# Grouped-query attention with a KV cache: a reordered head, an earlier last K load, and a rearranged tail

## Chip, cores and metric

One core of one Trainium2 chip runs the whole program. The metric is the device time of one execution in microseconds (us). Of the 16 executions of before, 15 lie within 0.3% of their median and all within 0.53% of one another, so differences below one microsecond are read from five rounds. The before median was 391.56 us over 5 runs.

## The reference

```python
# x (32,4,1024); k_cache, v_cache (32,4,2048,128); wq (1024,4096); wo (4096,1024); all bf16
q = (x @ wq).reshape(B, Sq, 32, 128).transpose(0, 2, 1, 3)
k = jnp.repeat(k_cache, 8, axis=1)
v = jnp.repeat(v_cache, 8, axis=1)
p = softmax(einsum("bhqd,bhkd->bhqk", q, k) * 128 ** -0.5)
o = einsum("bhqk,bhkd->bhqd", p, v)
out = o.transpose(0, 2, 1, 3).reshape(B, Sq, 4096) @ wo
```

The caches are 134 MB of the 151 MB that must be read. The kernel works in 32 "quads": quad q is one KV head (q // 8) and four batch entries, with one K tile and one V tile of 2 MB each.

## The kernel before

SyncE issues all loads in one queue. The order of the issues, and what each issue waits for, decide when data arrives (with K31 sent ahead of V29 and nothing else changed, its transpose started at 358.15 us instead of 361.65):

```python
for g in range(Hkv): sp_wq(g)
sp_K(0)
for q in range(NQ):                 # NQ = 32
    if q + 1 < NQ: sp_K(q + 1)      # two raw K buffers: K(q) waits for transpose kx(q-2)
    sp_V(q)                         # four V buffers: V(q) waits for PV of quad q-4
    if q in wo_at: sp_Wo(wo_at[q])
sp_Wo(Hkv - 1)
```

VectorE transposes K (`kx`) and takes the row maximum (`mx`). In its program the transpose for the next quad stands ahead of the maximum of this one, and the trace shows them run in that order (the transpose of K31 from 361.65 us, the maximum of quad 30 from 366.02):

```python
dve_trK(0)
for g in range(1, Hkv): qsb{g}      # scales half of Q projection g out of PSUM
for k in range(NQ + 1):
    if k + 1 < NQ: dve_trK(k + 1)   # kx1 also waits for "qp3", the fourth projection
    if k < NQ:     dve_max(k); dve_negm(k)
    if k >= 1:     dve_lred(k - 1); dve_recip(k - 1)
    ...
```

TensorE runs, per step k: scores S(k), transposes of the probabilities PT(k-1), the product PV(k-1), and the transpose OT(k-2). In the tail there are "fillers", matmuls whose results nobody reads:

```python
pe_qproj(0)
for me in range(4): pe_qt_round(0, me)
for g in range(1, Hkv): pe_qproj(g)       # each needs the PSUM banks of the one before
TF = 12,5,1,1,1,1
for k in range(NQ + 2):
    if k == NQ - 1: pe_fill(TF[0])        # twelve fillers before S(31)
    pe_S(k); ...
    if k == NQ: pe_fill(TF[1])
    pe_PT(k-1, 0); pe_PT(k-1, 1); ...; pe_PV(k-1, 0); ...; pe_PV(k-1, 1); ...; pe_OT(k-2)
pe_proj(Hkv - 1, 0); pe_proj(Hkv - 1, 1)  # last Wo; VectorE then adds acc and writes out
```

(`...` and the shortened loops are cuts.)

Of the kernel before, what the change touches and what calls it, by code (L numbers as in the profile page):

```python
# [5 lines left out]
F32 = mybir.dt.float32  # L6
U32 = mybir.dt.uint32
ACTF = mybir.ActivationFunctionType
ALU = mybir.AluOpType
# [51 lines left out]
def bass_standalone__gqa_block_cached__sampling_kernel(  # L61
# [9 lines left out]
    _, Hkv, Sk, Dh = k_cache.shape  # L71
    HD = wq.shape[1]
    Hq = HD // Dh
    REP = Hq // Hkv
# [5 lines left out]
    NQP = B // 4  # L80
# [13 lines left out]
    def sbt(name, shape, dt):  # L94
        t = nc.sbuf_tensor(name, shape, dt)
        sb.append(t)
        return t.__enter__()

    ident = sbt("ident", [128, 128], BF)
    xT = sbt("xT", [128, NDT, 128], BF)  # L100
    Qsb = sbt("Qsb", [128, HD], BF)
    Qrep = sbt("Qrep", [128, 4, REP, 128], BF)
# [55 lines left out]
    PJ_ps = PS[:, 7168:8192].bitcast(F32)  # L158
    PJ6_ps = PS[:, 6144:7168].bitcast(F32)
    FILL_ps = PS[:, 6144:7168].bitcast(F32)  # L160

    sems = []

# [60 lines left out]
    def sp_K(q):  # L224
        slot = q % 2
        k_uses[slot] += 1
        b0, g = quad_b0(q), quad_g(q)

        def aps():
            src = k_cache[b0:b0 + 4, g, :, :].rearrange("j (p n) d -> p j (n d)", p=128)  # L230
            dst = Kraw[:, slot, :].rearrange("p (j x) -> p j x", j=4)
            return dst, src
        waits = []
        if q >= 2:
            waits.append(f"kx{q - 2}")
        sp_dma(aps, s_K[slot], f"K{q}", 16 * k_uses[slot], waits)

    def sp_V(q):
        slot = q % NV
        v_uses[slot] += 1  # L240
        b0, g = quad_b0(q), quad_g(q)

        def aps():
            src = v_cache[b0:b0 + 4, g, :, :].rearrange("j (p n) d -> p j (n d)", p=128)
            dst = Vs[slot].rearrange("p (j x) -> p j x", j=4)
            return dst, src
        waits = []
        if q >= NV:
            waits.append(f"o{q - NV}")
        if slot >= 2 and v_uses[slot] == 1:  # L250
            waits.append("qp3")
        sp_dma(aps, s_V[slot], f"V{q}", 16 * v_uses[slot], waits, engname=v_eng, qidx=q)

    def sp_Wo(g):
        semh = s_w[0]
        w_uses[0] += 1

        def aps():
            src = wo[REP * Dh * g:REP * Dh * (g + 1), :].rearrange("(h d) n -> d h n", d=Dh)
            dst = Wo  # L260
            return dst, src
        waits = ["qp3"]
        if g >= 1:
            waits.append(f"proj{g - 1}_1")
        sp_dma(aps, semh, f"wo{g}", 16 * w_uses[0], waits)

    wo_at = {4: 0, 13: 1, 21: 2}
    for g in range(Hkv):
        sp_wq(g)
    sp_K(0)  # L270
    for q in range(NQ):
        if q + 1 < NQ:
            sp_K(q + 1)
        sp_V(q)
        if q in wo_at:
            sp_Wo(wo_at[q])
    sp_Wo(Hkv - 1)

    def sp_final(eng):
# [27 lines left out]

    qrep_events = {g: [] for g in range(Hkv)}
    qrep_items = {"dve": [], "act": [], "pool": []}
    g0_assign = ["dve", "act", "pool", "pool"] * 4  # L310
    idx = 0
    for me in range(4):
        for c in range(4):
# [20 lines left out]
                                 fill=1.0, base=0, pattern=[[-1, 128]], channel_multiplier=1)  # L334
    S.add("pool", "ident0", pool_memset)
    S.add("pool", "ident", pool_ident)
    if V_ON_POOL:
        later = {1: [], 2: [], 3: []}
        for item in qrep_items_pool_later:
            later[int(item[0][4])].append(item)  # L340
        v_after = {1: qrep_items["pool"] + later[1], 9: later[2], 17: later[3]}
        for q in range(NQ):
            S.add("pool", *pool_v_items[q])
            for item in v_after.get(q, []):
                S.add("pool", *item)
    else:
        for item in qrep_items["pool"] + qrep_items_pool_later:
            S.add("pool", *item)
# [27 lines left out]
    def pe_qproj(g):  # L376
        prev = (bank_free_ev[0] or ()) + (bank_free_ev[1] or ())
        bank_free_ev[0] = bank_free_ev[1] = (f"qsb{g}_dve", f"qsb{g}_act")

        def f(eng):  # L380
            waits = ["xT_ev", f"wq{g}"] + list(prev)
            S.wait(eng, "pe", *waits)
            ins = None
            for dt in range(NDT):
                for n2 in range(2):
                    ins = eng.matmul(QP_ps[:, 512 * n2:512 * (n2 + 1)], xT[:, dt, :],  # L386
                                     wq_v[:, g, dt, 512 * n2:512 * (n2 + 1)],
                                     start=(dt == 0), stop=(dt == NDT - 1))
            return ins
        S.add("pe", f"qp{g}", f)  # L390
# [112 lines left out]

    fill_rhs = QT4[:, 0, 0, 0:512]

    def pe_fill(n):
        def f(eng):
            ins = None
            for i in range(n):
                ins = eng.matmul(FILL_ps, ident[:, :], fill_rhs, start=True, stop=True)  # L510
            return ins
        if n > 0:
            S.add("pe", None, f)

    pe_qproj(0)
    for me in range(4):
        pe_qt_round(0, me)
    for g in range(1, Hkv):
        pe_qproj(g)
    proj_at = {}  # L520
    for gg in range(1, Hkv):
        proj_at[NQP * gg + 2] = (gg - 1, 0)
        proj_at[NQP * gg + 3] = (gg - 1, 1)
    TF = [int(v) for v in _os.environ.get("GQA_TAILFILL", "12,5,1,1,1,1").split(",")]
    TF += [0] * (6 - len(TF))
    for k in range(NQ + 2):
        if k < NQ:
            if k == NQ - 1:
                pe_fill(TF[0])
            pe_S(k)  # L530
            if k in qt_round_after_S:
                gq, me = qt_round_after_S[k]
                pe_qt_round(gq, me)
        if 1 <= k <= NQ:
            if k == NQ:
                pe_fill(TF[1])
            pe_PT(k - 1, 0)
            pe_PT(k - 1, 1)
            if k == NQ:
                pe_fill(TF[2])  # L540
            pe_PV(k - 1, 0)
            if k == NQ:
                pe_fill(TF[3])
            pe_PV(k - 1, 1)
        if 2 <= k <= NQ + 1:
            if k == NQ + 1:
                pe_fill(TF[4])
            pe_OT(k - 2)
        if k in proj_at:
            pe_proj(*proj_at[k])  # L550
    pe_fill(TF[5])
    pe_proj(Hkv - 1, 0)
    pe_proj(Hkv - 1, 1)

    def dve_xT_ev(eng):
        S.wait(eng, "dve", "xT_tr")
# [15 lines left out]
    S.add("dve", "qsb0_dve", dve_qsb(0))  # L572
    for item in qrep_items["dve"]:
        S.add("dve", *item)
    S.add("act", "qsb0_act", act_qsb(0))
    for item in qrep_items["act"]:
        S.add("act", *item)
# [56 lines left out]
    def dve_acc(g, n2):  # L634
        def f(eng):
            waits = [f"proj{g}_{n2}"]
            if (g, n2) != (0, 0) and not (g == Hkv - 1 and n2 == 1):
                pg, pn = (g, 0) if n2 == 1 else (g - 1, 1)
                waits.append(f"acc{pg}_{pn}" if not (pg == Hkv - 1) else "fin0")
            if g == Hkv - 1 and n2 == 1:  # L640
                waits.append("fin0")
            S.wait(eng, "dve", *waits)
            a = acc[:, 512 * n2:512 * (n2 + 1)]
            src = PJ_ps if proj_bank(g, n2) == 7 else PJ6_ps
            if g == 0:
                return eng.tensor_copy(a, src)
            if g < Hkv - 1:
                return eng.tensor_tensor(a, a, src, ALU.add)
            return eng.tensor_tensor(out_sb[:, 512 * n2:512 * (n2 + 1)], a, src, ALU.add)
        if g == Hkv - 1:  # L650
            name = f"fin{n2}"
        else:
            name = f"acc{g}_{n2}"
        S.add("dve", name, f)

    dve_trK(0)
    for g in range(1, Hkv):
        S.add("dve", f"qsb{g}_dve", dve_qsb(g))
    acc_at = {}
    for gg in range(1, Hkv):  # L660
        acc_at[NQP * gg + 2] = (gg - 1, 0)
# [1 line left out]
    for k in range(NQ + 1):  # L663
# [7 lines left out]
            dve_recip(k - 1)  # L671
        if k in acc_at:
            dve_acc(*acc_at[k])
    dve_acc(Hkv - 1, 0)
    dve_acc(Hkv - 1, 1)

    def act_qtev(gq, me):
        slot = gq % 2
# [20 lines left out]
            return eng.activation(Osb[:, :], O_ps, ACTF.Copy, scale=st_rl(slot))  # L699
        S.add("act", f"on{q}", f)  # L700

    def act_evac(q, half):
        def f(eng):
            waits = [f"pt{'AB'[half]}{q}"]
            if q >= 1:
                waits.append(f"o{q - 1}")
            S.wait(eng, "act", *waits)
            src = B4v if half == 0 else B5v
            return eng.activation(PTsb[:, 8 * half:8 * half + 8, :], src, ACTF.Copy)  # L709
        S.add("act", f"pte{'AB'[half]}{q}", f)  # L710

    def act_exp(q, c):
        slot = q % 2
# [12 lines left out]
    def act_otev(q):  # L726
# [10 lines left out]
            return eng.activation(dst, src, ACTF.Copy)  # L737
        S.add("act", f"ote{q}", f)

    for me in range(4):  # L740
        act_qtev(0, me)
    for g in range(1, Hkv):
        S.add("act", f"qsb{g}_act", act_qsb(g))
    for k in range(NQ + 2):
        if 2 <= k <= NQ + 1:
            act_norm(k - 2)
        if 1 <= k <= NQ:
            act_evac(k - 1, 0)
            act_evac(k - 1, 1)
        if k < NQ:  # L750
            for c in range(4):
                act_exp(k, c)
            if k in qt_round_after_S:
                gq, me = qt_round_after_S[k]
                act_qtev(gq, me)
        if 2 <= k <= NQ + 1:
            act_otev(k - 2)

    S.plan()
    with nc.Block() as block:  # L760
# [53 lines left out]
```

## Time and profile before

| what | before |
|---|---|
| median time | 391.56 us |
| span of the profiled run | 389.7 us |
| moved by DMA | 152.21 MB, mean 391 GB/s |
| where DMA falls short | first 3.5 us; 49 to 51.5 us; from about 368 us |
| K30 transpose starts / K31 transpose starts | 351.38 / 361.65 us |
| last projection starts | 382.99 us |

First the page of the profile. The strips have 40 slices of the span each: the TensorE clock that was granted in tenths (9 means full, 5 means half) and the rate of the DMA. The last line is the head of the chain of waits.

```profile
span 389.7 us, 10775 instructions
...
PEclk9985955896555556965556668996656557955699
...
GB/s 304 410 418 410 410 320 414 418 407 415 416 416 413 409 413 417 416 408 408 417 422 415 408 415 418 415 408 410 419 422 412 408 414 420 416 409 413 385 111 29
...
DMA 65%; DVE 21%; PE 7%; SPq 2%; ACT 2%; issue 0%
```

The rate is near 410 in nearly every slice. The sixth slice (about 49 to 58 us) has 320, and the last two have 111 and 29. The chain says that 65% of the span is spent waiting for K loads. No slice moves more than 422. With the same bytes to move at that rate, this kernel can gain only by closing holes in the DMA and by shortening what follows the last loads.

The hole in detail. This is the table of busy times by stretches of one microsecond; the last two columns are the DMA's share and its GB/s.

```profile
core 0: us, PE busy (x) PEld busy (x) DVE busy (x) ACT busy (x) POOL busy (x), PEclk, DMA share, GB/s
...
48.00:49.00 1.00, 0.00 (x0) 0.00 (x0) 1.00 (x1) 0.00 (x0) 0.00 (x0) 1.00 1.04 414
49.00:50.00 1.00, 0.00 (x0) 0.00 (x0) 1.00 (x2) 0.00 (x0) 0.00 (x0) 0.83 0.09 25
50.00:51.00 1.00, 0.00 (x0) 0.00 (x0) 1.00 (x1) 0.00 (x0) 0.00 (x0) 0.50 0.00 0
51.00:52.00 1.00, 0.00 (x0) 0.00 (x0) 1.00 (x1) 0.00 (x0) 0.00 (x0) 0.50 0.79 270
...
```

What led to it is in the timeline (start, duration, engine, line, operation, then the idle time before it and who ended it). L587 is the K transpose, L386 a Q projection, L202 a load's issue.

```profile
29.26 4.45 DVE L587 STREAM_TRANSPOSE KX<-Kraw 128x4096 uint32<-128x4096 uint32 x1 [12.93 <-DMA Kraw<-in_k_cache_dram]
...
34.39 6.09 PE L386 MATMUL PS<-arena,xT 128*128 128x512 bf16 x16 [12.22 <-DVE Qsb L563]
...
41.30 3.61 PE L386 MATMUL PS<-arena,xT 128*128 128x512 bf16 x16 [0.83 <-DVE Qsb L563]
...
45.56 4.43 DVE L587 STREAM_TRANSPOSE arena<-Kraw 128x4096 uint32<-128x4096 uint32 x1
...
50.02 0.37 SPq L202 DMA_DIRECT2D Kraw<-in_k_cache_dram  x1
```

The second K transpose, at 45.56, was not late for want of data: K1 had landed at 34.4 us, as the landing records in the trace show (a load is split over 16 DMA engines, each with a record of its own; "landed" means that the last part is there). It waited for the fourth projection (41.30 to 44.9), which waited for the third, which waited for VectorE, which was transposing K0. K3 needed the buffer that the second transpose frees, and was issued at 50.02, when the queue had run dry.

The tail, again from the timeline. L598 is the maximum, L510 the fillers, L428 the scores, L498 the last projection.

```profile
351.38 4.45 DVE L587 STREAM_TRANSPOSE KX<-Kraw 128x4096 uint32<-128x4096 uint32 x1 [4.16 <-DMA Kraw<-in_k_cache_dram]
...
361.65 4.45 DVE L587 STREAM_TRANSPOSE arena<-Kraw 128x4096 uint32<-128x4096 uint32 x1 [3.08 <-DMA Kraw<-in_k_cache_dram]
...
366.02 2.25 DVE L598 TENSOR_REDUCE stat<-PS 128x1 f32<-128x2048 f32 x1
...
367.04 2.79 PE L510 MATMUL PS<-QT,ident 128*128 128x512 bf16 x12
```

```profile
369.76 2.67 PE L428 MATMUL PS<-arena,QT 32*32 32x512 bf16 x64
...
372.47 2.29 DVE L598 TENSOR_REDUCE stat<-PS 128x1 f32<-128x2048 f32 x1 [3.63 <-PE PS L428]
...
382.99 3.63 PE L498 MATMUL PS<-arena,OT_all 128*128 128x512 bf16 x16 [0.15 <-ACT OT_all L737]
```

The line at 361.65 waited 3.08 us for K31. The maximum of quad 30 (366.02) stands behind that transpose in VectorE's program, although the scores it reads were ready at 363. Twelve fillers ran from 367.04 to 369.8, and only then the scores of quad 31.

### The profile page before, as it was taken

The page shows a single profiled execution, that of the slowest core. Times are in us where ns is not written, and L with a number is a line of the kernel's source. Part 1 is how long each engine was busy: PE and PEld are TensorE (multiplying, and loading weights), DVE is VectorE, ACT ScalarE, POOL GpSimd, SP SyncE. Part 2 cuts the span into 40 slices and gives each one's busy share as a digit, 9 for nine tenths or more (in the row PEclk, how much of TensorE's full clock was granted, in tenths as well). Part 3 has the DMA queues.
Part 4 walks back from the last instruction along what each step waited for, and adds up shares of the span by engine and source line. Part 5 has one row for each costly group of instructions (what it writes and reads, how often), then busy time and mean ns, then how long its engine had stood idle before and what let it go on. Part 6 is the DMA issues. An engine that isn't in the chain of part 4 may idle for free.

```text
span 389.7 us, 10775 instructions
## 1 busy us (share of the span) xinstructions
PE 274.7 (71%) x4925; PEld 169.1 (43%) x4925; DVE 237.2 (61%) x177; ACT 184.3 (47%) x409; POOL 20.4 (5%) x62
## 2 busy tenths in 40 slices
PE   1724759957577769788656769757557779776976
PEld 1311336634345446455434445435334445354542
DVE  0205498773676567777356667767276667767731
ACT  1410136954445555555344555655335555554471
POOL 0304000005000000005000000000000000000000
PEclk9985955896555556965556668996656557955699
DMA  8999989999999999999999999999999999999920
GB/s 304 410 418 410 410 320 414 418 407 415 416 416 413 409 413 417 416 408 408 417 422 415 408 415 418 415 408 410 419 422 412 408 414 420 416 409 413 385 111 29
DMA packets 42589, 152.21 MB, mean 391 GB/s; under 512 B 1200, under 2 KB 1456, under 8 KB 42544
## 3 DMA queue, kind: packets, MB, share of 16 engines
q1 hardware_dynamic: 42544, 151.52, 96.7%
q8 instruction: 39, 0.64, 0.6%
q14 instruction: 6, 0.05, 0.0%
HBM read 151.26 MB, written 0.26 MB: 389 GB/s over the span
## 4 chain that ended last, share of the span: by engine, by line
DMA 65%; DVE 21%; PE 7%; SPq 2%; ACT 2%; issue 0%
DMA Kraw<-in_k_cache_dram 65%; DVE KX L587 18%; PE PS L386 2%; SPq L202 2%; PE PS L428 2%; DVE stat L598 1%; DVE arena L587 1%; ACT PTsb L709 1%; PE PS L498 1%; ACT Psb L722 1%; PE PS L466 1%; PE PS L510 1%; PE PS L454 1%; DVE Qsb L563 1%; ACT OT_all L737 0%
## 5 line engine op out<-in xcount | busy, mean ns | idle before, releaser
L722 ACT ACTIVATE Psb<-PS,stat 128x512 bf16<-128x512 f32 x128 | 86.2, 687 | 91.8 <-DVE stat L609 91.8
L587 DVE STREAM_TRANSPOSE KX<-Kraw 128x4096 uint32<-128x4096 uint32 x16 | 71.1, 4445 | 56.0 <-DMA Kraw<-in_k_cache_dram 56.0
L587 DVE STREAM_TRANSPOSE arena<-Kraw 128x4096 uint32<-128x4096 uint32 x16 | 71.1, 4443 | 50.2 <-DMA Kraw<-in_k_cache_dram 50.2
L709 ACT ACTIVATE PTsb<-PS 128x1024 bf16<-128x1024 bf16 x64 | 62.0, 1021 | 68.8 <-PE PS L454 68.8
L428 PE MATMUL PS<-arena,QT 32*32 32x512 bf16 x1024 | 55.8, 529 | 39.0 <-ACT Psb L722 38.8
L428 PE MATMUL PS<-KX,QT 32*32 32x512 bf16 x1024 | 57.9, 542 | 33.9 <-ACT Psb L722 28.4
L598 DVE TENSOR_REDUCE stat<-PS 128x1 f32<-128x2048 f32 x32 | 72.2, 2256 | 4.7 <-PE PS L428 4.7
L454 PE MATMUL PS<-ident,Psb 128*128 128x128 bf16 x512 | 53.9, 289 | 1.4 <-ACT Osb L699 1.4
L454 PEld LDWEIGHTS PS<-ident,Psb 128*128 128x128 bf16 x512 | 47.2, 135 | 17.1 <-issue 12.7
L428 PEld LDWEIGHTS PS<-arena,QT 32*32 32x32 bf16 x1024 | 25.8, 108 | 60.4 <-DVE stat L631 35.5
L428 PEld LDWEIGHTS PS<-KX,QT 32*32 32x32 bf16 x1024 | 26.3, 109 | 56.1 <-DVE stat L631 35.9
L466 PE MATMUL PS<-V,PTsb 128*32 128x128 bf16 x1024 | 29.3, 294 | 4.5 <-ACT PTsb L709 4.5
L466 PE MATMUL PS<-arena,PTsb 128*32 128x128 bf16 x1024 | 25.4, 262 | 9.4 <-ACT PTsb L709 8.9
L386 PE MATMUL PS<-arena,xT 128*128 128x512 bf16 x64 | 18.5, 454 | 17.3 <-DVE Qsb L563 13.1
L305 POOL COPY Qrep<-Qsb 128x256 bf16<-128x256 bf16 x56 | 19.7, 405 | 162.6 <-PE PS L403 132.8
L466 PEld LDWEIGHTS PS<-V,PTsb 128*32 128x32 bf16 x1024 | 23.2, 132 | 11.0 <-ACT PTsb L709 9.1
L466 PEld LDWEIGHTS PS<-arena,PTsb 128*32 128x32 bf16 x1024 | 19.4, 116 | 15.7 <-ACT PTsb L709 13.9
L722 ACT ACTIVATION_READ_ACCUMULATOR Psb<-PS,stat 128x1 f32 x128 | 26.2, 205 | 0.0
L386 PEld LDWEIGHTS PS<-arena,xT 128*128 128x128 bf16 x64 | 6.9, 112 | 28.2 <-issue 24.0
L569 ACT ACTIVATE Qsb<-PS 128x512 bf16<-128x512 f32 x4 | 2.4, 597 | 35.5 <-PE PS L386 35.5
L688 ACT ACTIVATE QT<-PS 128x1024 bf16<-128x1024 bf16 x16 | 16.2, 1037 | 0.4 <-PE PS L403 0.4
L498 PE MATMUL PS<-arena,OT_all 128*128 128x512 bf16 x64 | 15.3, 385 | 0.2 <-ACT OT_all L737 0.2
(28 smaller groups left out, 100.2 us busy)
## 6 DMA issues: line engine op xcount, KB each, us to landing
Kraw<-in_k_cache_dram SPq DMA_DIRECT2D x32, 2048.0 KB, 15.9
V<-in_v_cache_dram SPq DMA_DIRECT2D x16, 2048.0 KB, 20.6
arena<-in_v_cache_dram SPq DMA_DIRECT2D x16, 2048.0 KB, 20.4
arena<-in_wq_dram SPq DMA_DIRECT2D x4, 2048.0 KB, 14.5
arena<-in_wo_dram SPq DMA_DIRECT2D x4, 2048.0 KB, 23.7
Qrep<-in_x_dram SPq DMA_DIRECT2D x1, 256.0 KB, 2.8
out_dram<-PTsb SPq DMA_DIRECT2D x2, 128.0 KB, 1.7
```

The lines of the kernel that those rows point to most:

```text
L202: ins = eng.dma_start(dst, src)
L305: return eng.tensor_copy(dst, src)
L386: ins = eng.matmul(QP_ps[:, 512 * n2:512 * (n2 + 1)], xT[:, dt, :], wq_v[:, g, dt, 512 * n2:512 * (n2 + 1)], start=(dt == 0), stop=(dt == ...
L428: ins = eng.matmul(S_ps[32 * j:32 * (j + 1), 512 * c:512 * (c + 1)], lhsT, rhs, start=(me == 0), stop=(me == 3), tile_position=(32 * c, 32 ...
L454: ins = eng.transpose(dst[:, tt, :], p_cols_ap(t), ident[:, :])
L466: ins = eng.matmul(O_ps[32 * j:32 * (j + 1), :], PTsb[:, t, 32 * j:32 * (j + 1)], vv[:, j * Sk + t * Dh:j * Sk + (t + 1) * Dh], start=(t = ...
L498: ins = eng.matmul(dst_ps, OT_all[:, h, :], Wo[:, hh, 512 * n2:512 * (n2 + 1)], start=(hh == 0), stop=(hh == REP - 1))
L587: return eng.transpose(KXs[q % 2].bitcast(U32), Kraw[:, q % 2, :].bitcast(U32))
L598: return eng.tensor_reduce(st_m(slot), S_ps[:, :], AX.X, ALU.max)
L688: return eng.activation(dst, src, ACTF.Copy)
L709: return eng.activation(PTsb[:, 8 * half:8 * half + 8, :], src, ACTF.Copy)
L722: return eng.activation(p_exp_out_ap(c), S_ps[:, 512 * c:512 * (c + 1)], ACTF.Exp, bias=st_negm(slot), scale=1.0, accum_out=st_lsum(slot, c))
```

## The change

It has three parts. The head runs projections 1 and 2 before the Q transposes and takes POOL out of the first copies. The load of K31 goes ahead of V29. The tail gets other filler counts, one of the last two evictions on VectorE, and the accumulated output `acc` is folded into PSUM by two fp32 matmuls with an identity, so that the closing add becomes a copy.

```diff
-    g0_assign = ["dve", "act", "pool", "pool"] * 4
+    g0_assign = ["dve", "act"] * 8
     pe_qproj(0)
+    pe_qproj(1)
+    pe_qproj(2)
     for me in range(4):
         pe_qt_round(0, me)
-    for g in range(1, Hkv):
-        pe_qproj(g)
+    pe_qproj(3)
 # (evictions qsb1, qsb2 move the same way: ahead of the first K transpose)
+    KEARLY = 2        # the load of K31 moves up past KEARLY - 1 V loads: ahead of V29
-    TF = 12,5,1,1,1,1
+    TF = 4,4,0,0,2,2
+            if k == NQ - 2:
+                pe_fill(5)
             if k == NQ:
                 pe_fill(TF[1])
+                pe_proj_last_pre()      # PJ, PJ6 = ident32 x acc (fp32), start=True, stop=False
-    pe_proj(Hkv - 1, 0)
-    pe_proj(Hkv - 1, 1)
+    pe_proj_last_main(0)                # start=False: adds onto acc
+    pe_proj_last_main(1)
-            return eng.tensor_tensor(out_sb[...], a, src, ALU.add)
+            return eng.tensor_copy(out_sb[...], src)
-            act_evac(k - 1, 1)
+            if k < NQ:
+                act_evac(k - 1, 1)
+    act_evac(NQ - 1, 1, engname="dve")
+    # the second half of the output is now evicted by ScalarE ("fin1")
```

## The prediction

> **What bounds the kernel now.** The DMA. The page gives 152 MB at a mean of 391 GB/s over a span of 389.7 us, and the busy table by stretches shows about 410 GB/s with a DMA share of 1.0 nearly everywhere. It falls short in the first 3.5 us, at 49 to 51.5 us (24, 0, 270 GB/s) and after about 368 us. The chain of waits is 65% K loads and 18% the transposes (L587) that follow them. So only that hole and the tail behind the last K tile can give time.
>
> **The hole (before: about 2.1 us).** K3 is issued at 50.02 us (timeline) because its buffer comes free only when the second K transpose ends (45.56 to 50.0 us). K1 had landed at 34.4, but that transpose waits for the fourth Q projection (41.3 to 44.9), which waits behind VectorE's first K transpose (29.26 to 33.7). The change runs projections 1 and 2 before the Q transposes and before K0 lands; the fourth should end near 29 us, so the second transpose starts near 34.4 and K3 is issued near 39 us. The hole closes: every later K landing moves about 2.1 us earlier. Taking POOL out of the first Qrep copies is neutral.
>
> **The tail (before: K30 starts transposing at 351.38, K31 lands at 361.63, end 389.7).** VectorE does transpose K31 before the maximum of quad 30, so that maximum (366.02) waits for K31's landing: 361.65 + 4.4. The change sends K31 ahead of V29, one 2 MB load (5.1 us) earlier, so K31 no longer limits. VectorE's own sequence does: K30 transpose 4.45, maximum 2.3, small operations 0.5, K31 transpose 4.45 = 11.7 us after K30 lands, instead of 14.7. That is 3.0 us. The last Wo (landing 376.7 before) keeps about 3 us of slack.
>
> **The end.** Evacuating the second half of PT on VectorE beside ScalarE: about 0.35 us. Folding acc into PSUM removes almost nothing: the closing add took 0.69 us, a ScalarE eviction of that shape 0.60. Against this, two fp32 matmuls on TensorE. [...] the idle gap there is about 2.7 us minus four fillers (0.9), so I estimate up to 0.4 us of delay. Net about 0.
>
> **The clock.** The last 22 us of before ran at full clock, after twelve fillers at 367. [...]
>
> **Sum.** 2.1 + 3.0 + about 0.1 = 5.2 us: 391.56 to 386.3 us, range 385.0 to 389.0. Faster by over 2% (below 383.7): 0.05. Within 2%: 0.945. Slower: 0.005.
>
> **What would show it.** No DMA hole near 50 us, and S0 near 35 us instead of 45.7; K30's transpose at about 349.2; K31 transposed with no DMA wait before it, starting right after quad 29's reciprocal; maximum of quad 30 at about 361; [...] full clock from about 356; end near 384.5.
>
> **What would make it wrong.** The 16 DMA engines drift apart (landing spread of the last K loads is 8 us): if the slowest one was already late at the hole, it gains only about 0.5 us. A clock at half through S31, or slower fp32 matmuls, would eat the tail's gain.

## The result and the profile after

The changed kernel took 385.50 us median (385.32 to 386.96, 9 runs); before took 391.69 us (390.45 to 392.53, 16 runs). The ratio is 0.9844, 95% interval 0.9831 to 0.9857. A ratio here is the mean time of one kernel's runs over that of the other's of the same rounds, so it is not quite the ratio of the medians. Executions over 1.5% slower than the fastest of the same kernel are left out of the means. The span of the profiled run fell from 389.7 to 384.1 us, where 384.5 had been predicted.

The page after: the sixth slice is full. A smaller dip (333) has appeared in slice 36.

```profile
span 384.1 us, 10770 instructions
...
PEclk9996555666565567966655556976556666965799
...
GB/s 302 409 415 412 409 412 416 413 409 415 415 415 413 409 412 417 417 409 408 418 420 416 409 412 419 415 410 409 419 421 415 409 411 418 417 333 406 419 296 29
...
DMA 68%; DVE 18%; PE 7%; SPq 4%; ACT 2%; issue 0%
```

The former hole, in the table by stretches:

```profile
...
49.00:50.00 1.00, 0.74 (x20) 0.47 (x22) 1.00 (x1) 1.00 (x2) 0.00 (x0) 0.50 1.00 397
50.00:51.00 1.00, 1.00 (x48) 0.86 (x43) 1.00 (x2) 0.52 (x1) 0.00 (x0) 0.50 1.01 401
...
```

The timeline of the head, with L415 the projections, L653 the K transpose, L457 the scores and L204 a load's issue:

```profile
24.66 3.62 PE L415 MATMUL PS<-arena,xT 128*128 128x512 bf16 x16
...
30.85 4.45 DVE L653 STREAM_TRANSPOSE KX<-Kraw 128x4096 uint32<-128x4096 uint32 x1 [7.08 <-DMA Kraw<-in_k_cache_dram]
...
35.97 4.45 DVE L653 STREAM_TRANSPOSE arena<-Kraw 128x4096 uint32<-128x4096 uint32 x1
...
36.13 3.85 PE L457 MATMUL PS<-KX,QT 32*32 32x512 bf16 x64 [7.85 <-DVE Qsb L627]
...
40.44 0.37 SPq L204 DMA_DIRECT2D Kraw<-in_k_cache_dram  x1
```

The fourth projection is done at 28.3 us. The second K transpose follows the first at once (35.97 for 45.56), and K3 is issued at 40.44 for 50.02. The transpose of K30, 300 us later, starts at 349.30 for 351.38: the 2.1 us that the hole had cost.

The timeline of the tail (L697 is the reciprocal, L664 the maximum, L541 the fillers, L566 the fp32 matmuls, L579 the last projection):

```profile
349.30 4.45 DVE L653 STREAM_TRANSPOSE KX<-Kraw 128x4096 uint32<-128x4096 uint32 x1 [3.00 <-DMA Kraw<-in_k_cache_dram]
...
356.32 0.17 DVE L697 RECIPROCAL stat<-stat 128x1 f32<-128x1 f32 x1
356.40 4.43 DVE L653 STREAM_TRANSPOSE arena<-Kraw 128x4096 uint32<-128x4096 uint32 x1
...
360.75 2.25 DVE L664 TENSOR_REDUCE stat<-PS 128x1 f32<-128x2048 f32 x1
...
363.76 1.03 PE L541 MATMUL PS<-QT,ident 128*128 128x512 bf16 x4
...
364.72 2.48 PE L457 MATMUL PS<-arena,QT 32*32 32x512 bf16 x64
...
367.24 2.29 DVE L664 TENSOR_REDUCE stat<-PS 128x1 f32<-128x2048 f32 x1 [3.67 <-PE PS L457]
...
371.62 1.88 PE L566 MATMUL PS<-acc,ident 128*128 128x512 f32 x4
...
377.52 3.63 PE L579 MATMUL PS<-arena,OT_all 128*128 128x512 bf16 x16
```

The K31 transpose follows a reciprocal with no wait. (The prediction calls it that of quad 29; by the program's order it is that of quad 28, `dve_recip(k - 1)` of step k = 29.) The maximum of quad 30 comes 11.45 us after K30's transpose starts (360.75 - 349.30); before it was 14.64 us (366.02 - 351.38). That is 3.2 us. The last projection starts at 377.52 for 382.99.

The new dip at 340 to 347 us costs nothing. K31 must wait for the transpose of K29 (done at 343.5), and the DMA engines that run ahead have finished K30 by then: by the landing records the first of the 16 had it at 341.0 and the last at 349.3. The last one sets the pace, and it never ran dry: K31's last part landed 5.1 us after K30's, one load's time. The run with the head alone has no such dip, and its last load (Wo) landed at 374.42 us, here at 374.35.

### The profile page after: what moved, and what is told of

Its sections match the earlier page's. It is cut to its first block, busy times and chain, and to the rows that moved or that the text cites. A ratio compares the mean times of both kernels' runs of the same rounds, so it can differ in the third digit from the quotient of the medians.

```text
span 384.1 us, 10770 instructions
## 1 busy us (share of the span) xinstructions
PE 277.9 (72%) x4925; PEld 172.0 (45%) x4925; DVE 237.3 (62%) x181; ACT 185.5 (48%) x413; POOL 17.8 (5%) x56
## 4 chain that ended last, share of the span: by engine, by line
DMA 68%; DVE 18%; PE 7%; SPq 4%; ACT 2%; issue 0%
DMA Kraw<-in_k_cache_dram 68%; DVE arena L653 17%; SPq L204 4%; PE PS L457 2%; PE PS L495 2%; ACT PTsb L773 1%; PE PS L541 1%; PE PS L579 1%; PE PS L483 1%; DVE stat L664 1%; PE PS L566 0%; PE PS L507 0%; ACT Psb L787 0%; ACT PTsb L831 0%; ACT OT_all L802 0%
## 5 line engine op out<-in xcount | busy, mean ns | idle before, releaser
L653 DVE STREAM_TRANSPOSE KX<-Kraw 128x4096 uint32<-128x4096 uint32 x16 | 71.1, 4445 | 53.5 <-DMA Kraw<-in_k_cache_dram 53.5
L653 DVE STREAM_TRANSPOSE arena<-Kraw 128x4096 uint32<-128x4096 uint32 x16 | 71.1, 4444 | 53.1 <-DMA Kraw<-in_k_cache_dram 53.0
L773 ACT ACTIVATE PTsb<-PS 128x1024 bf16<-128x1024 bf16 x63 | 61.1, 1021 | 72.5 <-PE PS L483 72.5
L457 PE MATMUL PS<-KX,QT 32*32 32x512 bf16 x1024 | 59.9, 570 | 40.9 <-ACT Psb L787 29.7
L457 PE MATMUL PS<-arena,QT 32*32 32x512 bf16 x1024 | 57.0, 546 | 39.2 <-ACT Psb L787 39.2
L664 DVE TENSOR_REDUCE stat<-PS 128x1 f32<-128x2048 f32 x32 | 72.1, 2253 | 3.7 <-PE PS L457 3.7
L483 PEld LDWEIGHTS PS<-ident,Psb 128*128 128x128 bf16 x512 | 49.3, 139 | 15.3 <-issue 12.4
L483 PE MATMUL PS<-ident,Psb 128*128 128x128 bf16 x512 | 55.9, 296 | 0.0
L457 PEld LDWEIGHTS PS<-KX,QT 32*32 32x32 bf16 x1024 | 26.8, 112 | 64.5 <-DVE stat L697 36.7
L457 PEld LDWEIGHTS PS<-arena,QT 32*32 32x32 bf16 x1024 | 26.3, 110 | 61.4 <-DVE stat L697 37.4
L324 POOL COPY Qrep<-Qsb 128x256 bf16<-128x256 bf16 x48 | 16.6, 400 | 163.3 <-PE PS L432 163.3
L415 PE MATMUL PS<-arena,xT 128*128 128x512 bf16 x64 | 16.0, 408 | 6.0 <-DMA arena<-in_wq_dram 4.3
L432 PEld LDWEIGHTS PS<-ident,Qrep 128*128 128x128 bf16 x128 | 10.5, 124 | 9.5 <-issue 9.3
L432 PE MATMUL PS<-ident,Qrep 128*128 128x128 bf16 x128 | 13.5, 276 | 0.0
L415 PEld LDWEIGHTS PS<-arena,xT 128*128 128x128 bf16 x64 | 6.4, 103 | 15.0 <-issue 6.7
```

The source lines that it names most:

```text
L324: return eng.tensor_copy(dst, src)
L415: ins = eng.matmul(QP_ps[:, 512 * n2:512 * (n2 + 1)], xT[:, dt, :], wq_v[:, g, dt, 512 * n2:512 * (n2 + 1)], start=(dt == 0), stop=(dt == ...
L432: ins = eng.transpose(bv[:, hh, :], Qrep[:, me, hh, :], ident[:, :])
L457: ins = eng.matmul(S_ps[32 * j:32 * (j + 1), 512 * c:512 * (c + 1)], lhsT, rhs, start=(me == 0), stop=(me == 3), tile_position=(32 * c, 32 ...
L483: ins = eng.transpose(dst[:, tt, :], p_cols_ap(t), ident[:, :])
L653: return eng.transpose(KXs[q % 2].bitcast(U32), Kraw[:, q % 2, :].bitcast(U32))
```

## The experiments

Five rounds each, in four groups on four chips (the first four runs of the table; "all but the end"; the next four; the last three), always with before in the same rounds. So ratios, and not medians, are compared from one group to another. Ratios are to before; the changed kernel has 0.9844.

| run | edit | median us | ratio (95%) |
|---|---|---|---|
| head alone | before + head | 390.16 | 0.9955 (0.9939 to 0.9971) |
| K31 early alone | before + load order | 389.99 | 0.9964 (0.9943 to 0.9984) |
| fillers alone | before + filler counts | 392.06 | 1.0006 (0.9985 to 1.0027) |
| K31 early and fillers | before + both | 389.21 | 0.9936 (0.9915 to 0.9956) |
| all but the end | before + head + K31 + fillers | 386.25 | 0.9862 (0.9845 to 0.9878) |
| no fold | changed, without the fold | 385.59 | 0.9853 (0.9827 to 0.9878) |
| no fold, fillers | the same, 8 fillers in its place | 385.69 | 0.9843 (0.9827 to 0.9860) |
| no split | changed, both last evictions on ScalarE | 385.99 | 0.9852 (0.9836 to 0.9869) |
| no fillers before S30 | changed, without those five | 386.61 | 0.9867 (0.9851 to 0.9884) |
| POOL back | changed, POOL in the first copies | 385.40 | 0.9846 (0.9824 to 0.9867) |
| K30 early too | changed + K30 ahead of V28 | 383.66 | 0.9794 (0.9777 to 0.9811) |
| K30 early, fillers moved | the same + six fillers before S29, four for five before S30 | 384.05 | 0.9802 (0.9785 to 0.9818) |

### The head alone

```diff
-    for me in range(4): pe_qt_round(0, me)
-    for g in range(1, Hkv): pe_qproj(g)
+    pe_qproj(1); pe_qproj(2)
+    for me in range(4): pe_qt_round(0, me)
+    pe_qproj(3)          # and the evictions, and POOL out of the copies
```

> The kernel before with the reordered projections alone (no POOL in the first copies, projections 1 and 2 before the Q transposes). Theory A (the hole stops all 16 DMA engines, and the last K landings set the end): no hole near 50 us, K30 lands about 2.1 us earlier than 351.4, total 2.1 us less (about 389.5). Rival B (only the slowest DMA engine counts, and it was late at the hole already): the hole goes, but the total falls by 0.5 us or less.

Measured: 390.16 us, 0.45% less, which is 1.8 us. No hole remained, and K30 landed at 349.25 instead of 351.36, so all of the 2.1 us reached the last K loads. The other profiles agree: in the four without the head K30 landed at 351.0 to 352.3, in the eight with it and K30 in its old place at 349.1 to 349.3. Rival B falls, but its premise did hold: in the run of before one engine was late at the hole already (1.85 us between the first and the last landing of V1), and the hole covered this, for K3 landed on all 16 within 0.34 us. So K3 gained only 0.8 us (56.24 for 57.08). The gain was whole again by K30, because the gap between the first and the last engine had by then grown to the same size in both runs (8.07 and 8.10 us); the last section has more on these gaps.

A part of the gain was then lost on TensorE. In the profiled execution the maximum of quad 30 started 2.3 us earlier than before (363.73 for 366.02), but that of quad 31 only 1.4 us (371.03 for 372.47): the twelve fillers, at half clock until 367.1, kept TensorE until 368.7.

### K31 early, alone

```diff
+        if q == NQ - 3:
+            sp_K(NQ - 1)      # K31 right after K30, before V29
```

> The kernel before with K31 loaded ahead of V29, nothing else; the old twelve fillers stay before the last score matmuls. Theory A of the prediction (VectorE's sequence is the limit once K31 is early): the maximum of quad 30 starts at 363.0 instead of 366.0 and the total falls by 3.0 us. Rival B (TensorE is the next limit: it ends quad 29's PV at 367.0 at half clock and then runs twelve fillers until 369.8): the maximum moves by 3 us, the score matmuls of quad 31 do not, and the total falls by 0.5 us or less.

Measured: 0.36% less, 1.4 us, between the two theories. The timeline shows which one holds (L589 transpose, L600 maximum, L512 fillers, L430 scores):

```profile
358.15 4.43 DVE L589 STREAM_TRANSPOSE arena<-Kraw 128x4096 uint32<-128x4096 uint32 x1
...
362.70 2.29 DVE L600 TENSOR_REDUCE stat<-PS 128x1 f32<-128x2048 f32 x1
...
366.41 2.75 PE L512 MATMUL PS<-QT,ident 128*128 128x512 bf16 x12
...
369.09 2.30 PE L430 MATMUL PS<-arena,QT 32*32 32x512 bf16 x64
...
371.43 2.29 DVE L600 TENSOR_REDUCE stat<-PS 128x1 f32<-128x2048 f32 x1 [5.87 <-PE PS L430]
```

The maximum of quad 30 moved by 3.3 us, from 366.02 to 362.70. The scores of quad 31 moved by 0.7 us, from 369.76 to 369.09, and ended 1.0 us earlier (371.4 for 372.4): TensorE was still busy, and then ran its twelve fillers from 366.41. So the limit passed to TensorE at once, as rival B had it, though B's 0.5 us was too little. The prediction's "VectorE's own sequence does" holds in the changed kernel, which also has thinner fillers (see below), and not here. The expected 3.0 us did not come from the load order alone.

### The fillers alone, and both together

```diff
-    TF = 12,5,1,1,1,1
+    TF = 4,4,0,0,2,2
+            if k == NQ - 2:
+                pe_fill(5)
```

> The kernel before with the new counts of filler matmuls alone (five before the scores of quad 30, then 4,4,0,0,2,2 for 12,5,1,1,1,1). Both theories: K31 still lands at about 361.6, so the maximum of quad 30 stays at 366 and the total changes by less than 0.5 us, less filler time near the end included. If fillers by themselves were the gain, 2 us or more would show here.

Measured: no change (1.0006). While K31 is late, fewer fillers gain nothing.

> The kernel before with K31 early and the new fillers together. Theory A: 3.0 us less, as with K31 alone. Rival B (the two need each other): 2.5 to 3.0 us less here, while each alone gives 0.5 or less; the scores of quad 30 run at full clock and those of quad 31 start about 3 us earlier than 369.8.

Measured: 389.21 us, 2.5 us less, but with a wide spread: 388.17, 388.36, 389.06, 389.35, 390.40 and 390.45. The best two are 3.7 and 3.9 us under the 392.02 of before in these rounds. Neither theory is met as it stands: the sum is B's, but one of the two parts alone had already given 1.4 us, and in the profile the scores of quad 30 ran mostly at half clock (3.81 us). The profiled execution was one of the worst two (390.45), and its clock shows at least a part of why. Lines of the table by stretches; the column before the DMA's share is the granted clock:

```profile
364.00:368.00 4.00, 3.74 (x80) 2.92 (x79) 2.34 (x4) 3.47 (x7) 0.00 (x0) 0.51 1.02 414
...
376.00:380.00 4.00, 2.45 (x68) 2.17 (x72) 0.32 (x2) 2.68 (x6) 0.00 (x0) 0.77 0.05 18
```

The clock was at half (0.51) while TensorE worked towards the scores of quad 31, which started at 368.69 although quad 30's first exponential was out by 367.0; and it fell again (0.77) after the scores of quad 31. Of the other executions only the time and the mean clock over the whole run are known, and the mean tells nothing here (0.695 in the fastest, 0.710 in the slowest but one), so it is an inference that their clocks in the tail differed.

### All but the end

This is before with the head, K31 early and the fillers; without the fold and the split eviction.

> The kernel before with the head, K31 early and the new fillers, so the changed kernel without the fold and without the split eviction. The parts measured alone (1.9, 2.5 and 0.35 us) fall short of the whole by about 1.4 us. Theory A (the parts simply add once the clock stays up; the run of K31 with fillers alone was pulled up by executions in which the clock fell in the tail): most executions near 385.9 us (the changed kernel plus 0.35), some at 387 to 388.5 in which the profile, if it catches one, shows half clock after the scores of quad 31. Rival B (fold and split are worth more together than one by one): all executions at 387 us or more, also with the clock up.

Measured: 386.25 us, all four executions within 386.21 to 386.39, and a full clock in the profile from 356 us to the end. That is 0.75 us over the changed kernel: 0.4 us more than theory A said, and below rival B's 387. The head, added to the run before, brought 3.0 us here and 1.8 us alone; the difference of 1.2 us is about the distance from that run's median to its best execution (388.17), which lies 1.9 us above this one. That the clock in the tail is the reason is likely, not shown. Why the clock fell so often there and not here was not settled.

### The fold and the split

```diff
-                pe_proj_last_pre()
-    start=False in the last projection; copies to out_sb
+    start=(hh == 0); VectorE adds acc to both halves
```

> The changed kernel without the fold of acc into PSUM: no fp32 matmuls, the closing adds back on VectorE; the split eviction stays. Theory A of the prediction (the fold is worth about nothing, its matmuls even delay PT of quad 31 by up to 0.4 us): within 0.4 us of the changed kernel, ratio to before 0.983 to 0.986. Rival B [...]: 0.5 to 1.5 us slower than the changed kernel in the executions in which the clock falls after the scores of quad 31, so a wider spread, ratio 0.986 to 0.989.

Measured: four of five executions at 385.39 to 385.67, as fast as the changed kernel, and one at 387.99, the profiled one. Two of its stretches; the second is the one in which PV of quad 31 and the last transposes run:

```profile
364.00:368.00 4.00, 3.78 (x80) 1.87 (x73) 0.00 (x0) 2.38 (x8) 0.00 (x0) 0.72 1.04 414
...
376.00:380.00 4.00, 3.65 (x71) 2.15 (x73) 0.19 (x1) 0.89 (x4) 0.00 (x0) 0.57 0.01 4
```

The same stretches of the changed kernel:

```profile
364.00:368.00 4.00, 4.00 (x84) 2.23 (x82) 0.76 (x1) 2.65 (x10) 0.00 (x0) 1.00 1.04 417
...
376.00:380.00 4.00, 3.81 (x30) 1.52 (x19) 0.54 (x1) 0.81 (x3) 0.00 (x0) 1.00 0.02 4
```

In this one execution the clock was lower twice: before the scores of quad 31 (0.72; the maximum of quad 31 then started at 368.54 for 367.24) and again in PV of quad 31 (0.57), where TensorE had idled without the fp32 matmuls (for 1.68 us before PT of quad 31 at 374.41; in the changed kernel PT at 373.33 follows the fp32 matmuls with no idle time). The execution took 2.4 us more than the run's median, of which the late maximum is 1.3. In the others nothing was lost. So the fold is worth about nothing, as predicted; whether it makes that fall rarer cannot be said from one case, and one of the changed kernel's nine executions (386.96) was long too.

```diff
-    TF = 4,4,0,0,2,2
+    TF = 4,12,0,0,2,2     # with the fold taken out
```

> As the run without the fold, but with eight more filler matmuls where the two fp32 matmuls stood (1.7 us of plain work whose result nobody reads). Theory A: as without the fold, or up to 0.4 us slower. Rival B: as fast as the changed kernel within 0.3 us, with its narrow spread[...].

Measured: 385.69 us, all five within 385.39 to 385.78. Eight plain fillers do as well as the two fp32 matmuls. Both expectations allow this; it only confirms that no time comes from folding as such.

```diff
-            if k < NQ:
-                act_evac(k - 1, 1)
-    act_evac(NQ - 1, 1, engname="dve")
+            act_evac(k - 1, 1)
```

> The changed kernel with both halves of the last PT eviction on ScalarE again. Theory A: the second half of PV of quad 31 starts about 0.3 us later and the total rises by 0.35 us (ratio 0.985). Rival: no visible change (below 0.15 us), if TensorE or the clock sets that stretch; or more than 0.8 us[...].

Measured: 385.99 us, 0.5 us more, with a full clock from 356 us on. The ratio, 0.9852, is what theory A gave. The split eviction is worth its 0.35 us or a little more.

### The five fillers before the scores of quad 30

```diff
-            if k == NQ - 2:
-                pe_fill(5)
```

> The changed kernel without the five fillers before the scores of quad 30. Theory A ([...] TensorE at half clock would be the limit in front of the scores of quad 31): scores of quad 30 at half clock (3.84 us for 2.96), scores of quad 31 start 1 to 2 us later than 364.7, total 1 to 2 us more. Rival B (VectorE's sequence is the limit whatever TensorE does): total within 0.4 us.

Measured: 386.61 us, 1.1 us more. The timeline (L457 scores of quads 30 and 31):

```profile
357.02 3.81 PE L457 MATMUL PS<-KX,QT 32*32 32x512 bf16 x64 [2.03 <-ACT Psb L785]
...
365.93 2.27 PE L457 MATMUL PS<-arena,QT 32*32 32x512 bf16 x64
```

The scores of quad 30 ran mostly at half clock (3.81 us for 2.96), and those of quad 31 started at 365.93 instead of 364.72. What theory A expected came, at the lower end of its range: five matmuls of no use save one microsecond. Why they do is shown only in part. The clock records show that without the five the clock was full all the same from 354.82 to 358.23; TensorE idled from 355.0 to 357.0, and then the clock was half until 365.06. In the changed kernel it was full from 356.91 to 360.33 and again from 363.74. So the clock rose without these fillers as well; whether they keep it from falling is not shown, for each kernel has one profile.

### POOL back in the first copies

```diff
-    g0_assign = ["dve", "act"] * 8
+    g0_assign = ["dve", "act", "pool", "pool"] * 4
```

> The changed kernel with POOL again taking half of the first Qrep copies. Theory A of the prediction (neutral): the Q transposes wait for POOL no longer than for the second projection that now runs ahead of them, the fourth projection ends by 30 us either way, total within 0.2 us. Rival: the head's gain came from taking POOL out; then the second K transpose starts late again and up to 2 us are lost.

Measured: 385.40 us (385.35 to 385.44, and one of 386.86), no difference (0.9846). The second K transpose started at 35.89 us, as in the changed kernel. The head's gain is the order of the projections alone.

### Going further: K30 early as well

```diff
+    item = order.pop(order.index("K30"))
+    order.insert(order.index("V28"), item)
```

> The changed kernel with K30 also sent one load earlier (ahead of V28), fillers as they are. K30 should land near 344.2 instead of 349.3. Theory A (VectorE's sequence is the limit): the maximum of quad 30 moves from 360.75 to 358.9, total 1.9 us less (ratio 0.9795). Rival B (TensorE at half clock is the limit: it ends quad 28's PV at 354.8 and the five fillers at 357): the scores of quad 30 still start at 357.0, the maximum moves by 0.7 us at most, total within 0.8 us of the changed kernel.

Measured: 383.66 us, ratio 0.9794, correct: 1.8 us less than the changed kernel and 2.1% under before (the interval, 0.9777 to 0.9811, includes 2%). The timeline (L656 transpose, L460 scores, L667 maximum, L582 last projection):

```profile
346.07 4.43 DVE L656 STREAM_TRANSPOSE KX<-Kraw 128x4096 uint32<-128x4096 uint32 x1
...
354.53 4.45 DVE L656 STREAM_TRANSPOSE arena<-Kraw 128x4096 uint32<-128x4096 uint32 x1 [1.06 <-DMA Kraw<-in_k_cache_dram]
...
356.63 2.24 PE L460 MATMUL PS<-KX,QT 32*32 32x512 bf16 x64
...
358.92 2.29 DVE L667 TENSOR_REDUCE stat<-PS 128x1 f32<-128x2048 f32 x1
...
375.50 3.63 PE L582 MATMUL PS<-arena,OT_all 128*128 128x512 bf16 x16
```

K30's transpose now starts when VectorE is free, at 346.07, without a wait. K31's transpose is again the one that waits for its load (1.06 us). The maximum of quad 30 starts at 358.92 for 360.75. The scores of quad 30 ended at 358.87, so TensorE and VectorE arrive together: rival B failed because the clock had risen at 356.3, so that these scores took 2.24 us.

> As the run with K30 early, and six fillers before the scores of quad 29 (TensorE idles there from 343.6 to 346.9), four instead of five before those of quad 30. If the clock then rises before 350, TensorE is no limit: scores of quad 30 start near 354.5, maximum of quad 30 at 358.9, total 1.9 to 2.3 us less than the changed kernel (ratio 0.978 to 0.980). If the clock does not rise, no better than with K30 early alone. The last Wo still lands at 374.3, so the final projection cannot start before that, and nothing below 382.3 us is possible this way.

Measured: 384.05 us, no better. The clock rose at 342.46, just before the six fillers began (342.51), but fell back at 349.3, and the scores of quad 29 still took 3.41 us. With K30 early alone the last Wo landed at 374.5 and the last projection started at 375.50: about one microsecond is left on this path before the loads themselves bound the end.

## Why the prediction was right

- **"Only that hole and the tail ... can give time."** Right. The steady part of the profile after runs at the same 410 GB/s.
- **The hole, 2.1 us.** Right in the landings: K30 came 2.1 us earlier in the head-only run and in the changed kernel. The time fell by 1.8 us in the run alone. A detail was off: K3 was issued at 40.44, not near 39, and the scores of quad 0 began at 36.13, not near 35. K0 landed 1.6 us later than before (30.8 for 29.2): 15 engines had it by 29.3, one at 30.8.
- **The tail, 3.0 us.** The size was right: 14.64 us became 11.45 us. The account was incomplete. It spoke of VectorE's sequence as the next limit; the run with K31 alone showed TensorE as the next limit, because of the twelve old fillers. The distance from the maximum of quad 30 to that of quad 31 tells the two apart. It is 6.49 us in the changed kernel (367.24 - 360.75) and 6.48 or 6.49 in the four other profiles in which the clock did not fall again (no fold with fillers, no split, POOL back, all but the end), where the scores of quad 31 started up to 0.6 us earlier; so there TensorE does not set it. With K31 alone it is 8.73 (371.43 - 362.70). The thinner fillers were part of the change but not of the prediction's argument for this term, so it was right partly by luck. The changed kernel with the twelve fillers back was not run.
- **The end, net zero for the fold, 0.35 us for the split.** Right: without the fold nothing changed in four of five executions, and without the split 0.5 us was lost. The two fp32 matmuls took 1.88 us at full clock: a bf16 matmul of 512 columns took 0.227 us, the fp32 one 0.94 us, 4.1 times as long. Before has no fp32 matmul, so the delay of up to 0.4 us was the author's estimate, which no run had shown. PT of quad 31 started 0.75 us after the last copy to Osb began, 0.2 us later than before (373.33 after 372.58; 378.34 after 377.80).
- **The clock.** Half right. The clock rose at 356.9, but "full clock from about 356" did not hold in the profiled execution: it was half again from 360.3 to 363.7. That cost nothing visible, because the scores of quad 31 still ended at 367.20, and at 367.16 to 367.19 in three profiles with a full clock throughout (no split, POOL back, all but the end). That fillers raise the clock is not shown: in before it rose at 367.10, when the first of the twelve (367.04) had hardly begun.
- **The sum.** 386.3 us predicted, 385.5 us measured, inside the range of 385.0 to 389.0. The last projection moved by 5.5 us (382.99 to 377.52) and the span by 5.6 us: 2.1 from the hole, 3.2 from K31, and 0.2 to 0.3 from the rest. The medians differ by 6.2 us; the profiled execution of before (391.35) was 0.3 us under its median, and that of the changed kernel (385.69) 0.2 us over its own.

## What to carry to other kernels

When the DMA is the bound, look for the few microseconds in which it does not run, and ask which small wait kept the next load from being issued; here a projection that a K transpose did not need for its data. In the tail, an engine's program order can make ready work wait for a load (the scores of quad 30 were ready at 363 us, their maximum started at 366.02): send the load earlier, but look at what the other engines do in that window, because the next limit may be close behind: here it was on TensorE. Fillers are not free: twelve in the wrong place ate about half of one improvement (1.4 us of the expected 3.0 were left), and five in an idle gap were worth one microsecond.

## What else the traces show

- The granted clock. In the traces of before and of the changed kernel every recorded stretch of one clock that ends within the span lasts 3.41 us or a multiple of it (3.41 to 54.61 us). What sets the rise is not shown: before, TensorE was busy from 359.14 us with gaps of no more than 0.3 us, and the clock rose only at 367.10, after 8 us; the whole stretch from 360.27 to 363.69 was busy (scores and transposes) and ended at half clock. Busy time in the trace alone thus does not foretell the rise in this case.
- Transposes on TensorE. The 16 transposes of one PT took 1.07 us at the full granted clock (quad 30 in before, 372.37) and 1.89 us at half (quad 29, 362.92).
- The fp32 matmuls. Each of the two 128x512 fp32 matmuls is recorded as two MATMULs (four for the two), 1.88 us in all at full clock.
- The 16 DMA engines of the core drift apart over the kernel. The first and the last landing of one 2 MB load were 0.2 us apart for K0 and 8.07 us for K30 (before). The gap grows in steps of 1.1 to 1.6 us in before and of 1.2 to 1.5 us in the changed kernel, while each trace shows 39 instruction packets of 16 KB, about 1 us each, spread over the run. The two go together: in both profiles each step follows an instruction packet, and from one step to the next there are eight packets (in the changed kernel the 1st, 9th, 17th, 25th and 33rd packet; in before the 2nd, 10th, 18th, 26th and 34th); only at the hole before has one step more, at the 1st packet (49.1 us). The trace does not name the engine of a packet, so that they cause the steps is likely, not shown.
